# Sequence transform with the tables stationary, so that z comes by token at once

## The chip, the cores and the metric

The kernel runs on one core of one Trainium2 chip. The metric is device time in microseconds (us) of one execution, taken as the median of repeated runs. The core has five engines with queues of their own: TensorE (PE in the profile, its weight loads PEld), VectorE (DVE), ScalarE (ACT), GpSimd (POOL) and SyncE (SP), which here issues DMAs. ACT issues a few DMAs too. SBUF is the working memory of 128 partitions; PSUM, in eight banks, is what TensorE writes to.

## The reference, cut to what matters

```python
def _attn_ref(x):                       # x: 8 x 3072 x 256
    X = np.fft.fft(x, axis=1)           # sequence transform
    X = np.fft.fft(X, axis=2)
    return X.real

def _moe_ref(x, w_in, w_out):           # w_in 256 x 2048, w_out 2048 x 256
    h = x @ w_in
    return (h - np.tanh(h)) @ w_out

def _moe2_ref(x, phi, w1, w2):          # phi 256 x 32, 8 experts of 4 slots
    logits = x @ phi
    d = softmax(logits over tokens)
    slot_input = d.T @ x
    ...                                 # small expert MLPs on 32 slots
    c = softmax(logits over slots)
    return c @ slot_out

reference(x, ...) = _moe2_ref(_moe_ref(_attn_ref(x).reshape(8 * 3072, 256), ...), ...)
```

The second transform (over 256 columns) and the residual form of the middle stage are folded into weights before the main loop, so that the loop needs `z`, the sequence transform of `x`, and applies the wide weights to `z`.

## The kernel before, in words

**Stages.** A head (to about 100 us) loads and folds the weights. The main loop goes over 8 batches of 12 tiles of 128 tokens. A tail from about 1275 us runs the experts and writes the output from saved logits.

**The sequence transform** has two steps. `dft24(b)` adds and subtracts the 24 slices of a batch in the buffer `xb` (operations "P" at L337 on POOL, "A" at L341 on ACT). Since x is real, a slice can hold both sides of the transform: the columns 0 to 128 of a slice hold cosine sums, the columns 129 to 255 sine sums, and column 128 belongs to the cosine side. Then `z_dft(i)` multiplies two slices `U` and `V` with the tables `C` and `Sn` of one tile (L421 to L424) on TensorE.

**One tile before.** `z_dft` has the slices stationary and streams the tables, so its PSUM bank `zps` holds z with columns on partitions (two halves of 128 columns, by 128 tokens). Its halves are columns 0 to 127 and 128 to 255, while the cosine side ends with column 128: so `trade` in `dft24` exchanges column 128 of `U` and `V` by three small ACT copies over `tC` (or `tD`), 15 of them a batch. From `zps`, `z_high` (L451, ACT) makes a rounded float32r copy and `z_low` (L455, DVE) the rest; both lie in the tile `zh`. `z_copy` (L441, ACT) copies `zps` to `z32`, `z_turn` (L460) transposes it on TensorE to `tps`, and `z_turned` (L464, ACT) copies that to `zts`, z by token.

**Four groups of a tile.** A tile has four groups g of 512 wide columns. `wide(g, 0)` and `wide(g, 1)` (L472) are three matmuls each, into `pp` and `qq`, with `zh` stationary. `evac` (L486, DVE) makes `pb` from `pp` and the column `zts[:, 129]`; `plus` (L491, DVE) makes the first half of `h` from `pb` and `qq`, `minus` (L494, POOL) the second from `pb` and the first. `act_h` (L499) is the tanh, back to PSUM, `act_t` (L507) its scaled float16 copy in the ring `tr`, `low_t` (L511, DVE) the float16 rest. Then `turn_t` (L515) issues one DMA transpose of 512 KB on SP's queue, `tt<-tr`, and `logits(g)` (L566, for a tile's first group L559 and L560 ahead of it, with `zh`) uses `tt` as stationary. For a pair of tiles softmax steps follow (L597 to L678), and `slots(i)` (L674, `ta<-tr,dh`) for a tile.

**Rings.** `zh` has 2 buffers, `zts` 5, `tt` 4, `pb` 3, `h` 2; `pp` and `qq` may hold 3 banks each of 7 that all share.

**Order.** Nothing is scheduled at run time: a planner (`Flow`) sets each engine's order when the program is built. Each operation has a due time (the offsets `SCHED` in units of groups, `4 * i + SCHED[...]` for a tile) and costs by engine; the planner takes, within a window of 40 operations, what can begin first. The loads of the next batch's `x` (8 a batch, issued by ACT at L307) are due every `XSTEP` groups. Each engine then runs its instructions strictly in that order.

Of the kernel before, what the change touches and what calls it, by code (L numbers as in the profile page):

```python
# [9 lines left out]
F32 = mybir.dt.float32  # L10
# [37 lines left out]
SCHED = {
    "soft_t": 13.585, "logits": 6.021, "slots": 16.891, "soft_d": 14.305, "z_slots": 16.295, "z_turn": -2.11,
    "wide0": -0.087, "wide1": 0.708, "z_dft": -5.872, "ls_sum": 13.142, "soft_m": 13.838, "soft_h": 15.611,  # L50
    "soft_l": 16.611, "z_acc": 20.073, "evac": 2.52, "z_high": -4.001, "z_low": -3.917, "z_copy": -3.035,
    "z_turned": 2.466, "low_t0": 5.48, "low_t1": 5.512, "plus": 2.954, "minus": 4.457, "soft_e": 13.941,
    "ls_keep": 13.542, "act_h0": 4.372, "act_h1": 5.168, "act_t0": 5.041, "act_t1": 5.277, "acc_add": 21.793,
    "soft_x": 13.523,
# [16 lines left out]
ZT = 5  # L71
# [164 lines left out]
def fft_mlp_softmoe_kernel(ctx: ExitStack, tc: tile.TileContext, x, w_in, w_out, phi, w1, w2, cq, fd, cm, ct, out):  # L236
# [33 lines left out]
    z3p = sbp("z3p", 1)  # L270
# [51 lines left out]
    tC = tmp.tile([128, 3, 4], F32, name="tC")  # L322
    tD = tmp.tile([128, 2], F32, name="tD")

    def dft24(b):
# [34 lines left out]
        c128 = slice(128, 129)  # L360

        def trade(sets, u, v, m):
            ns_, kk = sets.stop - sets.start, [("c", u)]
            ua, va = (lambda w=w: x4()[:, sets, w:w + m, c128] for w in (u, v))
            ta = lambda: tC[:, 0:ns_, 4 - u:4 - u + m, None]
            ku, kv = ([("x", b % 2, 8 * q + w + e) for q in range(sets.start, sets.stop) for e in range(m)] for w in (u, v))
            A(0, (kk, ta), (ku, ua), 1.0)
            A(0, (ku, ua), (kv, va), 1.0)
            A(0, (kv, va), (kk, ta), 1.0)

            vs = lambda: x4()[:, sets, v:v + m, 129:256]
            A(0.5 * ns_ * m, (kv, vs), (kv, vs), -1.0)

        for r in range(3):
            q = 8 * r
            t = tA if r % 2 == 0 else tB
            P(4, T(t, 0, 4), X(q, 4), X(q + 4, 4), add)
            P(4, X(q + 4, 4), X(q, 4), X(q + 4, 4), sub)
            P(2, X(q + 2, 2), T(t, 0, 2), T(t, 2, 2), sub)
            P(2, T(t, 0, 2), T(t, 0, 2), T(t, 2, 2), add)  # L380
            P(1, T(t, 2), X(q + 5), X(q + 7), sub)
            P(1, T(t, 3), X(q + 5), X(q + 7), add)
            A(2, T(t, 2, 2), T(t, 2, 2), float(np.sqrt(0.5)))
            P(1, X(q), T(t, 0), T(t, 1), add)
            P(1, X(q + 1), T(t, 0), T(t, 1), sub)
            P(2, X(q + 5, 2, 2), X(q + 4, 2, 2), T(t, 2, 2), add)
            P(2, X(q + 4, 2, 2), X(q + 4, 2, 2), T(t, 2, 2), sub)
            if r == 0:
                trade(slice(0, 1), 4, 6, 2)
                trade(slice(0, 1), 2, 3, 1)  # L390
                dft24.first = len(ops)
        for r, h, n, t in ((4, 6, 2, tA), (2, 3, 1, tB)):
# [21 lines left out]
    def z_dft(i):  # L414
# [38 lines left out]
    def z_low(i):  # L453
        z = zs[i]
        nv.tensor_tensor(out=z[2], in0=zpp[i], in1=z[1].bitcast(F32), op=ALU.subtract)  # L455

    def z_turn(i):
        tps = zpp[i] = halves(bank(f"zq{i}", "tps", 256))
        for k in range(2):
            nt.transpose(tps[:, k, :], zs[i][0][:, k, :], eye)  # L460
# [559 lines left out]
    hf.add({"A": 0.36}, lambda _: z_high(0), ["z0"], ["z2"])  # L1020
    hf.add({"V": 0.39}, lambda _: z_low(0), ["z0", "z2"], [("zh", 0)])
    hf.add({"A": 0.5}, lambda _: z_copy(0), ["z0", ("zh", 0), "clear"], ["z1"], free="B:zp0 B:sp0")
    hf.add({"T": 0.2}, lambda _: z_turn(0), ["z1"], ["z3"], take="B:zq0")
    hf.add({"A": 0.3}, lambda _: z_turned(0), ["z3"], [("zt", 0)], free="B:zq0")
# [190 lines left out]
    per_tile(z_high, {"A": 0.27}, lambda i: ([("zp", i)], [("zi", i)], "", ""))
    per_tile(z_low, {"V": 0.34}, lambda i: ([("zp", i), ("zi", i)], [("zh", i)], "", ""))
    per_tile(z_copy, {"A": 0.27}, lambda i: ([("zp", i), ("zh", i)], [("z", i)] + ["spec"] * (i % NQ == 0), "z32", f"z B:zp{i}" + f" B:sp{i}" * (i % NQ == 0)))
    per_tile(z_turn, {"T": 0.22}, lambda i: ([("z", i)], [("zq", i)], f"+B B:zq{i}", "z32"))
    per_tile(z_turned, {"A": 0.27}, lambda i: ([("zq", i), ("zh", i)], [("zt", i)], "zt", f"B:zq{i}"))
# [7 lines left out]
    stage(minus, n4, 1, {"G": 1.24}, lambda g: ([("pb", g), ("h", g, 0)], [("h", g, 1)], "", "pb"))  # L1227
# [15 lines left out]
    for g in sorted({*range(n4)} - {*by_pe}):  # L1243
        put(g + 0.001, {"D": 2.58}, lambda e, g=g: turn_t(g), [("t1", g, 0), ("t1", g, 1)], [("tt", g)], "tt", "", 2.4, "low_t1")
# [118 lines left out]
    fl = Flow({"B": 7, "w": WB, "v": WB, "z": 1, "a": 1, "z32": 1, "zh": 2, "zt": ZT, "pb": PB, "h": HB, "t": TB, "tt": 4, "L": 1, "dT": 1,  # L1363
# [322 lines left out]
```

## Time and profile before

| | us |
|---|---|
| median of 3 runs | 1377.36 |
| lowest and highest of them | 1374.88, 1383.24 |
| the profiled execution, first to last instruction (its span) | 1375.7 |
| PE, DVE, ACT, POOL busy in it | 1288.9, 1242.7, 1130.1, 1134.0 |

The page gives the profiled execution's span; no time around it is listed, and it lies 1.7 us under the median of the runs. A wait in the profile is the idle time of an engine ahead of one of its instructions, put down to what ended last. Matmuls overlap, so the duration of one is longer than what it takes from the next: the cost on the path is read from the starts.

### The profile page before, as it was taken

What the parts mean: (1) busy time and instruction counts of PE and PEld (TensorE: products, weight loads), DVE (VectorE), ACT (ScalarE), POOL (GpSimd) and SP (SyncE); (2) the same over time, 40 slices, a digit from 0 to 9 for tenths busy, and PEclk for the clock granted to TensorE, in tenths of its full rate; (3) what the DMA queues carried; (4) which work ended last, traced back from release to release, by engine and by line L of the source; (5) the groups of instructions that cost most, each with busy time, mean ns of one, the idle gap of its engine ahead of it and who ended that gap; (6) DMA issues with size and microseconds to landing.
All of it is one profiled execution on the core that took longest, in us unless ns stands there. A gap on an engine that the chain in (4) does not pass through costs nothing.

```text
span 1375.7 us, 37397 instructions
## 1 busy us (share of the span) xinstructions
PE 1288.9 (94%) x14155; PEld 939.9 (68%) x14155; DVE 1242.7 (90%) x2248; ACT 1130.1 (82%) x2520; POOL 1134.0 (82%) x869
## 2 busy tenths in 40 slices
PE   4888999999999899999999999999999999999895
PEld 3666676776777676777777767776777776667484
DVE  7789898999999898999999999999999999889394
ACT  3448887989999787998899889888899898787494
POOL 5956899999999898999999999999999994333352
PEclk9999999999999999999999999999999999999998
DMA  8349999999999999999999999999999999999989
GB/s 275 123 155 186 185 195 214 191 204 198 220 190 200 182 186 197 189 213 190 224 191 192 199 212 196 206 188 217 183 197 203 200 206 212 199 188 263 339 346 387
DMA packets 848483, 290.23 MB, mean 211 GB/s; under 512 B 793264, under 2 KB 837168, under 8 KB 847408
## 3 DMA queue, kind: packets, MB, share of 16 engines
q1 hardware_dynamic: 822192, 265.82, 102.1%
q10 hardware_dynamic: 26112, 22.03, 5.7%
q8 instruction: 111, 1.82, 0.5%
q14 instruction: 68, 0.56, 0.1%
HBM read 58.15 MB, written 30.67 MB: 65 GB/s over the span
## 4 chain that ended last, share of the span: by engine, by line
PE 69%; DMA 21%; DVE 4%; ACT 2%; issue 1%; POOL 1%; SPq 0%; DVEq 0%; ACTq 0%; POOLq 0%
DMA tt<-tr 20%; PE qq L472 16%; PE pp L472 15%; PE L L566 10%; PE ta L674 8%; PE tps L1594 3%; PE tps L460 1%; PE hps L911 1%; PE zlp L658 1%; PE zps L421 1%; PE zps L422 1%; PE zps L423 1%; PE zps L424 1%; PE hps L880 1%; PE L L559 1%
## 5 line engine op out<-in xcount | busy, mean ns | idle before, releaser
L494 POOL TENSOR_TENSOR h<-pb,h 128x512 f32<-128x512 f32 x384 | 495.6, 1296 | 130.4 <-DVE h L491 121.5
L499 ACT ACTIVATE th<-h 128x512 f32<-128x512 f32 x768 | 457.2, 611 | 78.5 <-DVE h L491 36.0
L511 DVE SCALAR_TENSOR_TENSOR tr<-th,tr 128x512 f16<-128x512 f32 x768 | 515.1, 682 | 3.8 <-ACT tr L507 2.8
L507 ACT ACTIVATE tr<-th 128x512 f16<-128x512 f32 x768 | 443.9, 603 | 7.4 <-DVE lsw L578 1.2
L472 PE MATMUL qq<-Wh,zh 128*128 128x512 f32 x768 | 337.5, 439 | 0.7 <-DVE tr L511 0.3
L472 PE MATMUL pp<-Wh,zh 128*128 128x512 f32 x768 | 324.1, 422 | 0.9 <-ACT tr L872 0.4
L486 DVE SCALAR_TENSOR_TENSOR pb<-W,zts,pp 128x512 f32<-128x512 f32 x384 | 283.8, 739 | 13.4 <-PE pp L472 6.3
L491 DVE SCALAR_TENSOR_TENSOR h<-pb,qq 128x512 f32<-128x512 f32 x384 | 260.8, 679 | 27.0 <-PE qq L472 16.6
L566 PEld LDWEIGHTS <-tt 128*128 128x128 f16 x6144 | 195.8, 96 | 105.8 <-DMA tt<-tr 55.3
L566 PE MATMUL L<-WPn,tt 128*128 128x64 f16 (+1 forms) x6144 | 231.0, 185 | 39.0 <-DMA tt<-tr 38.4
L472 PEld LDWEIGHTS pp<-Wh,zh 128*128 128x128 f32 x768 | 145.3, 189 | 69.5 <-issue 14.4
L472 PEld LDWEIGHTS qq<-Wh,zh 128*128 128x128 f32 x768 | 146.1, 190 | 28.9 <-issue 5.3
L472 PE MATMUL pp<-Wl,zh 128*128 128x512 f32 x384 | 152.6, 397 | 0.0
L472 PE MATMUL qq<-Wl,zh 128*128 128x512 f32 x384 | 152.3, 397 | 0.0
L674 PE MATMUL ta<-tr,dh 128*32 128x512 f16 x2304 | 143.0, 383 | 0.0
L337 POOL TENSOR_TENSOR xb<-xb 128x508 f32<-128x508 f32 (+3 forms) x98 | 137.7, 1409 | 5.4 <-DVE xb L337 5.0
L337 POOL TENSOR_TENSOR tA<-xb 128x1024 f32<-128x1024 f32 (+2 forms) x68 | 104.7, 1548 | 17.2 <-DMA xb<-in_x 15.0
L674 PEld LDWEIGHTS <-dh 128*32 128x32 f16 x2304 | 53.2, 96 | 75.6 <-issue 33.9
L337 POOL TENSOR_TENSOR xb<-tA 128x508 f32<-128x508 f32 (+2 forms) x77 | 82.1, 1073 | 0.2
L472 PEld LDWEIGHTS pp<-Wl,zh 128*128 128x128 f32 x384 | 73.4, 191 | 7.9
L337 POOL TENSOR_TENSOR tB<-xb 128x1024 f32<-128x1024 f32 (+1 forms) x45 | 71.8, 1602 | 8.3 <-DVE tB L337 7.6
L337 POOL TENSOR_TENSOR xb<-xb,tA 128x512 f32<-128x512 f32 (+1 forms) x46 | 77.2, 1678 | 0.2
(267 smaller groups left out, 1919.6 us busy)
## 6 DMA issues: line engine op xcount, KB each, us to landing
xb<-in_x ACTq DMA_DIRECT2D x24, 512.0 KB, 6.4
tr<-in_moe_w SPq DMA_DIRECT2D x16, 512.0 KB, 8.9
xb<-in_moe_w SPq DMA_DIRECT2D x12, 512.0 KB, 4.6
tt<-tr SPq DMA_TRANSPOSE x380, 5.6
raw<-in_moe_w_in SPq DMA_DIRECT2D x8, 512.0 KB, 6.1
raw<-in_moe_w_out SPq DMA_DIRECT2D x8, 512.0 KB, 4.2
xb<-in_x SPq DMA_DIRECT2D x8, 512.0 KB, 8.2
out<-tr SPq DMA_DIRECT2D x4, 1024.0 KB, 10.4
```

The costliest lines, as they stand in the source:

```text
L337: fn = lambda e: e.tensor_tensor(out=out[1](), in0=a[1](), in1=c[1](), op=op)
L421: nt.matmul(zps[:, 0, :], xb[:, U, 0:128], C, start=True, stop=False)
L472: nt.matmul(o, z, v, start=n == 0, stop=n == 2)
L486: nv.scalar_tensor_tensor(out=pb, in0=W128[:, c, :], scalar=zs[i][3][:, 129:130], in1=pqs.pop((g, 0)), op0=ALU.mult, op1=ALU.add)
L491: nv.scalar_tensor_tensor(out=hs[g][:, 0, :], in0=pbs[g], scalar=0.5, in1=pqs.pop((g, 1)), op0=ALU.mult, op1=ALU.add)
L494: ng.tensor_tensor(out=hs[g][:, 1, :], in0=pbs.pop(g), in1=hs[g][:, 0, :], op=ALU.subtract)
L499: ns.activation(out=o, in_=hs[g][:, k, :], func=AF.Tanh)
L507: ns.activation(out=place_t(g)[:, 0, k], in_=ths[g, k], func=AF.Copy, scale=T14)
L511: nv.scalar_tensor_tensor(out=t[:, 1, k], in0=ths.pop((g, k)), scalar=T14, in1=t[:, 0, k], op0=ALU.mult, op1=ALU.subtract)
L566: nt.matmul(L[:, pm].rearrange("p b s -> p (b s)")[:, 0:n], tt[:, hl, pm, f, :], WPn[:, 4 * c + f].rearrange("p b s -> p (b s)")[:, 0:n], ...
L674: nt.matmul(tas[p][32 * c:32 * c + 32, :], dhl[p][:, dl, 2 * k + pm, :], ts[c][:, tl, pm, :], start=(k == 0 and n == 0), stop=(i == tiles( ...
L1594: nt.matmul(o.rearrange("p r d -> p (r d)"), c[:, j, :], R[:, 3 * h + k:3 * h + k + 2, :].rearrange("p r d -> p (r d)"), start=(h == 0), s ...
```

## The change

`z_dft` now has the tables stationary and streams the slices, 129 columns for the cosine side and 127 for the sine side, so `zps` holds z by token. `z_copy` copies it to `zts` at once; `z_turn` transposes `zts` on TensorE, and `z_high` and `z_low` read the transposed bank. `z_turned` and the tile `z32` are gone, and so are the three copies of each `trade` (what is left, `turned`, is the change of sign that stood in it). A `zh` buffer is now taken at `z_turn` and no longer at `z_dft`; `zts` has 6 buffers. Planner costs of `z_turn`, `z_copy`, `minus` and the DMA transpose are higher, and all due times are new.

```diff
-XLEAD = 6.425
-XSTEP = 5.269
-XAT = -23.453
+XLEAD = 8.366
+XSTEP = 6.655
+XAT = -23.637
...
-    "wide0": -0.087, "wide1": 0.708, "z_dft": -5.872, "ls_sum": 13.142, "soft_m": 13.838, "soft_h": 15.611,
+    "wide0": -0.777, "wide1": -0.557, "z_dft": -7.091, "ls_sum": 12.873, "soft_m": 14.028, "soft_h": 16.03,
...
-ZT = 5
+ZT = 6
...
-        def trade(sets, u, v, m):
-            ns_, kk = sets.stop - sets.start, [("c", u)]
...
-            A(0, (kk, ta), (ku, ua), 1.0)
-            A(0, (ku, ua), (kv, va), 1.0)
-            A(0, (kv, va), (kk, ta), 1.0)
+        def turned(sets, v, m):
+            ns_ = sets.stop - sets.start
+            kv = [("x", b % 2, 8 * q + v + e) for q in range(sets.start, sets.stop) for e in range(m)]
             vs = lambda: x4()[:, sets, v:v + m, 129:256]
             A(0.5 * ns_ * m, (kv, vs), (kv, vs), -1.0)
...
-            nt.matmul(zps[:, 0, :], xb[:, U, 0:128], C, start=True, stop=False)
-            nt.matmul(zps[:, 0, :], xb[:, V, 0:128], Sn, start=False, stop=True)
-            nt.matmul(zps[:, 1, :], xb[:, U, 128:256], Sn, start=True, stop=False)
-            nt.matmul(zps[:, 1, :], xb[:, V, 128:256], C, start=False, stop=True)
+            nt.matmul(zps[:, 0:129], C, xb[:, U, 0:129], start=True, stop=False)
+            nt.matmul(zps[:, 0:129], Sn, xb[:, V, 0:129], start=False, stop=True)
+            nt.matmul(zps[:, 129:256], C, xb[:, V, 129:256], start=True, stop=False)
+            nt.matmul(zps[:, 129:256], Sn, xb[:, U, 129:256], start=False, stop=True)
...
-        zs[i][0] = z3p.tile([128, 2, 128], F32, tag="z32", name="z32")
-        ns.copy(out=zs[i][0], in_=zpp.pop(i))
+        zs[i] = [None, None, None, zts[:, i % ZT, :]]
+        ns.copy(out=zs[i][3][:, 1:257], in_=zpp.pop(i))
...
+            nt.transpose(tps[:, k, :], zs[i][3][:, 1 + 128 * k:129 + 128 * k], eye)
...
-    def z_turned(i):
-        zs[i][3] = zts[:, i % ZT, :]
-        ns.copy(out=zs[i][3][:, 1:257], in_=zpp.pop(i).rearrange("p a b -> p (a b)"))
...
-    stage(minus, n4, 1, {"G": 1.24}, lambda g: ([("pb", g), ("h", g, 0)], [("h", g, 1)], "", "pb"))
+    stage(minus, n4, 1, {"G": 1.29}, lambda g: ([("pb", g), ("h", g, 0)], [("h", g, 1)], "", "pb"))
...
-        put(g + 0.001, {"D": 2.58}, lambda e, g=g: turn_t(g), [("t1", g, 0), ("t1", g, 1)], [("tt", g)], "tt", "", 2.4, "low_t1")
+        put(g + 0.001, {"D": 2.72}, lambda e, g=g: turn_t(g), [("t1", g, 0), ("t1", g, 1)], [("tt", g)], "tt", "", 2.4, "low_t1")
```

**The order of the instructions, place 1.** On TensorE in the middle of the main loop, where the logits of a tile begin: the tile whose `zh` stands at L559 (L536 in the changed kernel) is one tile behind that of the wide matmuls. Before:

```order
L472 MATMUL qq_9095<-Wh_84,zh_8929 128x512
L472 MATMUL qq_9095<-Wl_85,zh_8929 128x512
L472 MATMUL qq_9095<-Wh_84,zh_8929 128x512
L472 MATMUL pp_9104<-Wh_84,zh_8929 128x512
L472 MATMUL pp_9104<-Wl_85,zh_8929 128x512
L472 MATMUL pp_9104<-Wh_84,zh_8929 128x512
L559 MATMUL L_8869<-Al_115,zh_8715 128x128
L560 MATMUL L_8869<-Al_115,zh_8715 128x2x32
```

The same place now:

```order
L449 MATMUL pp_9851<-Wh_84,zh_9681 128x512
L449 MATMUL pp_9851<-Wl_85,zh_9681 128x512
L449 MATMUL pp_9851<-Wh_84,zh_9681 128x512
L449 MATMUL qq_9859<-Wh_84,zh_9681 128x512
L449 MATMUL qq_9859<-Wl_85,zh_9681 128x512
L449 MATMUL qq_9859<-Wh_84,zh_9681 128x512
L536 MATMUL L_9631<-Al_112,zh_9478 128x128
L537 MATMUL L_9631<-Al_112,zh_9478 128x2x32
```

In both, the `pp` is that of the third group of its tile. Before, the `qq` ahead of it is that of the second group; now `pp` and `qq` of one group stand together, and the logits follow the `qq` of the third group.

**Place 2.** On ACT in the middle of the main loop, the copies of one tile between tanh (`th<-h`) and its float16 copy (`tr<-th`). Before:

```order
L499 ACTIVATE th<-h 128x512
L451 CAST zh<-zps 128x256
L507 ACTIVATE tr<-th 128x512
L499 ACTIVATE th<-h 128x512
L441 COPY z_9198<-zps 128x256
L507 ACTIVATE tr<-th 128x512
L499 ACTIVATE th<-h 128x512
L464 COPY zts<-tps 128x256
L507 ACTIVATE tr<-th 128x512
L499 ACTIVATE th<-h 128x512
L341 ACTIVATE xb_76<-tC 128x2
L507 ACTIVATE tr<-th 128x512
```

Now, at another tile (`zts<-zps` is the copy of a later tile than `zh<-tps`; the DMA is a load of the next batch's x):

```order
L422 COPY zts<-zps 128x256
L484 ACTIVATE tr<-th 128x512
L476 ACTIVATE th<-h 128x512 x2
L306 DMA xb_76<-in_x 128x2x256
L484 ACTIVATE tr<-th 128x512
L437 CAST zh<-tps 128x256
```

Two copies a tile are left of three, and the small copies over `tC` are gone; `zts` is written more than a tile ahead of its use.

**Place 3.** On TensorE in the changed kernel, between the transposes of a tile (`tps<-cms,zts`) and its first wide matmuls (`zh_9915`), a stretch with the slots of an earlier tile in it:

```order
L449 MATMUL pp_9896<-Wh_84,zh_9681 128x512
L431 MATMUL tps_9905<-cms_109,zts_105 128x128 x2
L449 MATMUL qq_9911<-Wh_84,zh_9681 128x512
...
L543 LDWEIGHTS tt_9819
...
L651 LDWEIGHTS dh_9730
...
L449 MATMUL pp_9973<-Wh_84,zh_9915 128x512
```

Before, this was the distance from a tile's `zps` to its first wide matmuls:

```order
L424 MATMUL zps_9149<-cqs_113,xb1_76 128x128
L472 MATMUL pp_9159<-Wh_84,zh_8929 128x512
...
L566 LDWEIGHTS tt_9031
...
L472 MATMUL qq_9190<-Wh_84,zh_8929 128x512
...
L472 MATMUL pp_9200<-Wh_84,zh_9167 128x512
```

What stands between the bank that `zh` is made from and the first use of `zh` is one `qq`, one block of logits and one of slots now, and was a `pp`, a block of logits and a `qq`; on the other tile of each pair it is a `pp`, a `qq`, a block of logits and two small softmax matmuls now.

## Rows read from the trace of the kernel before

**Rows 1.** Page, chain that ended last, shares of the span by engine and line

```profile
PE 69%; DMA 21%; DVE 4%; ACT 2%; issue 1%; POOL 1%; SPq 0%; DVEq 0%; ACTq 0%; POOLq 0%
```

**Rows 2.** Busy time by stage: PE, PEld, DVE, ACT, POOL, clock, DMA share, GB/s

```profile
100.00:1130.00 1030.00, 994.13 (x11478) 730.89 (x11478) 970.45 (x1747) 909.50 (x2050) 976.59 (x747) 0.99 1.14 198
1130.00:1275.00 145.00, 139.26 (x1726) 99.00 (x1724) 130.00 (x241) 117.10 (x251) 54.30 (x43) 1.00 1.11 218
```

**Rows 3.** TensorE's instructions in order of time: start, duration, line

```profile
1040.75 1.48 PE L674 MATMUL ta<-tr,dh 128*32 128x512 f16 x24
1042.16 0.50 PE L472 MATMUL pp<-Wh,zh 128*128 128x512 f32 x1
...
1042.97 0.60 PE L566 MATMUL L<-WPn,tt 128*128 128x64 f16 x16
1043.41 0.48 PE L472 MATMUL qq<-Wh,zh 128*128 128x512 f32 x1
...
1044.20 0.40 PE L472 MATMUL pp<-Wh,zh 128*128 128x512 f32 x1
...
1044.90 0.22 PE L559 MATMUL L<-Al,zh 128*128 128x128 f32 x1
```

**Rows 4.** Waits of the whole span: total us, times, longest us

```profile
PEld L566 <- DMA tt<-tr: 55.3, 61, 4.1
...
PE L L566 <- DMA tt<-tr: 38.4, 37, 3.9
...
DVE pb L486 <- ACT zts L464: 5.3, 8, 2.0
```

**Rows 5.** Waits from 100 to 1130 us

```profile
POOL h L494 <- DVE h L491: 45.7, 42, 3.4
...
PE L L566 <- DMA tt<-tr: 33.2, 29, 3.9
```

**Rows 6.** The tile tt: issue times min/median/max ns, landing times

```profile
L515 SPq DMA_TRANSPOSE tt<-tr x379: 1316/2651/5997, 102.4 to 1255.1; - x190
...
DMA to landing us min/median/max: 4.2/5.6/10.1
```

**Rows 7.** The longest such wait: timeline of ACT's, SP's and TensorE's queues

```profile
459.84 0.44 ACTq L307 DMA_DIRECT2D xb<-in_x  x1
...
463.09 6.00 SPq L515 DMA_TRANSPOSE tt<-tr  x1
...
469.46 0.82 PE L566 MATMUL L<-WPn,tt 128*128 128x64 f16 x16 [3.89 <-DMA tt<-tr]
...
471.68 2.75 PE L674 MATMUL ta<-tr,dh 128*32 128x512 f16 x24
```

**Rows 8.** Busy time in the 20 us around it, columns as in rows 2

```profile
460.00:470.00 10.00, 6.11 (x73) 5.05 (x73) 7.73 (x13) 7.98 (x18) 9.63 (x8) 0.90 1.24 159
470.00:480.00 10.00, 10.00 (x99) 6.43 (x96) 5.95 (x12) 4.13 (x9) 5.50 (x4) 0.75 0.93 180
```

**Rows 9.** Groups by form: count, busy us, mean ns, idle before

```profile
L464 ACT COPY zts<-tps 128x256 f32<-128x256 f32 x96 | 37.1, 387 | 12.1 <-PE tps L460 11.8
```

**Rows 10.** L341: small ACT copies, count, min/median/max ns

```profile
L341 ACT ACTIVATE tC<-xb x32: 187/205/282, 66.1 to 1134.5; 128x2 f32<-128x2 f32 x16, 128x1 f32<-128x1 f32 x8, 128x4 f32<-128x4 f32 x8
```

**Rows 11.** From a tile's zps to its first wide matmul, timelines of three engines

```profile
1046.50 0.38 PE L421 MATMUL zps<-cqs,xb 128*128 128x128 f32 x2
...
1047.17 0.39 PE L424 MATMUL zps<-cqs,xb 128*128 128x128 f32 x2
1047.31 0.47 PE L472 MATMUL pp<-Wh,zh 128*128 128x512 f32 x1
...
1049.33 0.40 PE L472 MATMUL pp<-Wh,zh 128*128 128x512 f32 x1
...
1048.23 0.37 ACT L451 CAST zh<-zps 128x256 fp32r<-128x256 f32 x1
...
1048.72 0.41 DVE L455 TENSOR_TENSOR zh<-zps,zh 128x256 fp32r<-128x256 f32 x1
```

**Rows 12.** POOL's work in the loop, 300 to 1100 us

```profile
L494 POOL TENSOR_TENSOR h<-pb,h 128x512 f32<-128x512 f32 x265 | 341.5, 1294 | 30.4 <-DVE h L491 26.3 <-ACT z L441 1.6 <-ACT tr L507 0.9
```

More of the change, by code (lines that the diff above doesn't have):

```diff
@@ L38 @@
 NQ = 12
-DSTEPS = 32.998
-XLEAD = 6.425
-XSTEP = 5.269
-XAT = -23.453
+DSTEPS = 33.347
+XLEAD = 8.366
+XSTEP = 6.655
+XAT = -23.637
 XBUSY = 1.25
 XLAT = 5.0
-XFIRST = 24.735
+XFIRST = 26.264
 SCHED = {
-    "soft_t": 13.585, "logits": 6.021, "slots": 16.891, "soft_d": 14.305, "z_slots": 16.295, "z_turn": -2.11,
-    "wide0": -0.087, "wide1": 0.708, "z_dft": -5.872, "ls_sum": 13.142, "soft_m": 13.838, "soft_h": 15.611,
[L51 to L54, printed above, removed]
+    "soft_t": 13.884, "logits": 5.754, "slots": 16.828, "soft_d": 14.997, "z_slots": 16.764, "z_turn": -6.044,
+    "wide0": -0.777, "wide1": -0.557, "z_dft": -7.091, "ls_sum": 12.873, "soft_m": 14.028, "soft_h": 16.03,
+    "soft_l": 16.693, "z_acc": 20.81, "evac": 1.167, "z_high": -5.502, "z_low": -4.279, "z_copy": -6.26,
+    "low_t0": 4.839, "low_t1": 5.286, "plus": 3.095, "minus": 3.3, "soft_e": 14.131,
+    "ls_keep": 12.969, "act_h0": 3.982, "act_h1": 3.863, "act_t0": 4.399, "act_t1": 4.607, "acc_add": 23.511,
+    "soft_x": 13.019,
 }
@@ L445, in z_copy, with z_turn @@
             ns.copy(out=spec[0:1, 1, b:b + 1], in_=sps[0:1, 1:2])
+    def z_turn(i):
+        tps = zpp[i] = halves(bank(f"zq{i}", "tps", 256))
+        for k in range(2):
+            nt.transpose(tps[:, k, :], zs[i][3][:, 1 + 128 * k:129 + 128 * k], eye)
     def z_high(i):
@@ L454, in z_low @@
         z = zs[i]
[L455 to L460, printed above, removed]
-    def z_turned(i):
-        zs[i][3] = zts[:, i % ZT, :]
-        ns.copy(out=zs[i][3][:, 1:257], in_=zpp.pop(i).rearrange("p a b -> p (a b)"))
+        nv.tensor_tensor(out=z[2], in0=zpp.pop(i), in1=z[1].bitcast(F32), op=ALU.subtract)
     hs, tq, tts, pqs, pbs, ths = {}, {}, {}, {}, {}, {}
@@ L1019, in fft_mlp_softmoe_kernel @@
     hf.add({"T": 1.0}, lambda _: z_dft(0), ["cq"] + x_keys(0), ["z0"], take="B:zp0 B:sp0")
[L1020 to L1024, printed above, removed]
+    hf.add({"A": 0.5}, lambda _: z_copy(0), ["z0", "clear"], ["z1", ("zt", 0)], free="B:zp0 B:sp0")
+    hf.add({"T": 0.3}, lambda _: z_turn(0), ["z1", "cms"], ["z3"], take="B:zq0")
+    hf.add({"A": 0.36}, lambda _: z_high(0), ["z3"], ["z2"])
+    hf.add({"V": 0.39}, lambda _: z_low(0), ["z3", "z2"], [("zh", 0)], free="B:zq0")
     hf.run()
@@ L1211, in k_dft @@
         n = i % NQ
-        return [("cq", n)] + x_keys(i), [("zp", i)], f"+B zh z B:zp{i}" + f" B:sp{i}" * (n == 0), ""
+        return [("cq", n)] + x_keys(i), [("zp", i)], f"+B z B:zp{i}" + f" B:sp{i}" * (n == 0), ""
     per_tile(z_dft, {"T": 0.9}, k_dft)
[L1215 to L1219, printed above, removed]
+    per_tile(z_copy, {"A": 0.3}, lambda i: ([("zp", i)], [("zt", i)] + ["spec"] * (i % NQ == 0), "zt", f"z B:zp{i}" + f" B:sp{i}" * (i % NQ == 0)))
+    per_tile(z_turn, {"T": 0.3}, lambda i: ([("zt", i)], [("zq", i)], f"+B zh B:zq{i}", ""))
+    per_tile(z_high, {"A": 0.27}, lambda i: ([("zq", i)], [("zi", i)], "", ""))
+    per_tile(z_low, {"V": 0.34}, lambda i: ([("zq", i), ("zi", i)], [("zh", i)], "", f"B:zq{i}"))
     n4 = last + 1
```

34 lines of the change are left out of this document (9 added, 25 removed).

## The prediction

> **What bounds the kernel now.** I read the chain that ended last first: 69% of it is TensorE and 21% DMA, nearly all of that the transposes `tt<-tr`; ACT has 2% [rows 1]. So the first question is not what ACT saves but what TensorE waits for. The busy times by stage come next. From 100 to 1130 us TensorE is busy for 994 of 1030 us, POOL for 976.6 and ACT for 909.5; after 1130 us POOL has little left to do (54 of 145 us), because the last batch needs no transform after it [rows 2]. A busy TensorE says little by itself, so I read its instructions in order of time: an undisturbed stretch has no hole. A block of slots takes 1.41 us (1040.75 to 1042.16), `pp` 0.81 behind it, a block of logits 0.44, `qq` 0.79 and the `pp` behind it 0.70 [rows 3]. The chain of TensorE is therefore dense, and its holes are in the list of waits: the logits waited 37 times, 38.4 us in total, for a DMA transpose (61 times, 55.3 us, on the side of the weight loads, which includes times in which matmuls still ran) [rows 4]. 33.2 us of the 38.4 fall before 1130 us [rows 5]. POOL's own waits in that stretch are 45.7 us, for `plus` [rows 5]: it runs at 95% and idles when the wide matmuls come late.
>
> Why do transposes come late? SP needs 2.65 us (median) to issue one of the 379 and up to 6.0; a transpose lands after 5.6 us, up to 10.1 [rows 6]. The longest wait shows the pattern: ACT issues a load of x at 459.84, the next transpose occupies SP for 6.0 us from 463.09, and at 469.46 the logits have waited 3.89 us [rows 7]. There TensorE stood idle for 4 us; the granted clock then was 0.75 on average from 470 to 480 us [rows 8], a mixture of 2.4 and 1.2 GHz, and a block of slots took 2.75 us where it takes 1.48 by the same kind of row [rows 3, 7]. Over 100 to 1130 us the clock is 0.99 [rows 2], so some 10 us of full speed are lost that way, part of them while TensorE waits anyway.
>
> **The change, part by part.**
>
> *ACT.* Gone are 96 copies `z_turned` at 387 ns, 37.1 us [rows 9], and 15 small copies a batch, 120 in all, at the 205 ns that 32 of them show [rows 10]: 24.6 us. Together 61.7 of ACT's 1130 us. The `z_copy` that stays writes `zts` instead of `z32`, the same 128 by 256 elements. As ACT has 2% of the chain, nearly all of the 61.7 us lie beside other work. On the path is what waited for `zts`: `evac` 8 times, 5.3 us [rows 4]; with `zts` written more than a tile ahead this goes. I take 3 us, between 0 and 5.3.
>
> *TensorE's work.* Four table matmuls a tile with 129, 129, 127 and 127 streamed columns in place of four with 128, and two transposes as before: the same 512 columns. The stationary loads are four either way. The twelfth tile of a batch has four matmuls in place of six small ones. I set this at 0; the bounds are 0 and a gain of 2 us. An odd count of columns is not in the trace; the four table matmuls of 128 columns take 0.81 us (1046.50 to 1047.31) [rows 11], so 0.2 us for 128 columns, and one more or less is nothing.
>
> *Logits later.* This is the main term. Counted over both orders, the logits of a group stand behind the `pp` of the same later group as before, but now also behind its `qq`, so that between `qq` of a group and its logits there are one more `qq` and one more block of logits: 0.79 + 0.44 = 1.23 us [rows 3]. The other end moves too: on DVE `low_t`, which the transpose waits for, has on average 0.12 to 0.17 of a group more of `plus` and `evac` ahead of it. A group takes 3.0 us (265 of them in 800 us [rows 12]), so 0.4 us of the 1.2 are used up there. A transpose gets 0.8 us more to land. Taken from 37 waits of 1.04 us on average this would be 30 us if each lost the full 0.8 and 0 if DMA simply landed later by as much; many waits are shorter than 0.8, and one that is shortened lets the next start earlier. I take 23 us.
>
> *Loads of x.* They are spread over 6.7 groups each in place of 5.3; in ACT's order the last four of a batch now take about 12 groups and took 9. Since the longest wait stood behind such a load [rows 7], fewer of them should pile up: 4 us, between 0 and 10.
>
> *Clock.* If the longest waits lose 0.8 us and some vanish, part of the 10 us comes back: 3 us, between 0 and 8.
>
> *z's path.* `zh` is now made from the transposed bank, so the head's first tile needs `z_copy` and the transposes ahead of `z_high`: the copy at 0.39 us [rows 9], the transposes at half of four table matmuls, 0.4 us [rows 11], and two hops between engines, once: +1 us. In the loop the cover decides. Before, from the last table matmul (1047.17 plus 0.39) to the end of `z_low` (1048.72 plus 0.41) were 1.57 us, and the first wide matmul of that tile began 0.20 us later, at 1049.33 [rows 11]: tight already. In the new order there are between the transposes and that matmul, on one tile of a pair, `qq`, logits and slots (0.79 + 0.44 + 1.41 = 2.6 us), on the other `pp`, `qq`, logits and two small matmuls (at least 0.70 + 0.79 + 0.44 = 1.9 us); before it was 0.81 + 0.44 + 0.79 = 2.0 us here [rows 3]. About the same, so 0; what it costs if the cover is too thin is a rival below.
>
> *POOL.* Its work in the loop stays. In the head four short operations move to it from DVE, at some 1 us each: at most 4 us, hidden if POOL is not late there.
>
> *Sum.* On TensorE's side −23 − 4 − 3 − 3 + 1 = −32 us. Before 1130 us POOL puts a ceiling on it: its work fills 976.6 of 1030 us, so at most 53 us can go, and of these 45.7 are waits for `plus` [rows 2, 5]. Two engines at 95% do not idle at the same moments, and what one of them gains the other gives back in part. I take two thirds: −21 us. The profiled execution spans 1375.7 us, the median of the runs is 1.7 above; 1377.4 − 21 gives 1356 us.
>
> **The rivals.**
>
> *No change.* POOL is the real bound up to 1130 us, and TensorE's waits only move: what it no longer waits for at the logits it waits for at `pp` and `qq`, whose banks come free when POOL's half of `h` has gone through ACT. For it: POOL's 95%, and that its work is not touched [rows 2]. Against it: of its 53 idle us 45.7 are waits for something that TensorE feeds [rows 5]. What remains is the last stretch, with 5.2 us of logits waits (38.4 − 33.2), and `evac`: 1372 to 1379 us. The Trainium skill, "Perfetto Trace Analysis", section "Identifying the Most-Contended Engine", judges TensorE's headroom by the share of its weight loads and would optimize the busiest engine first; here weight loads fill 731 of 1030 us, 71%, which leaves POOL as that engine and this change without an object [rows 2]. By the starts in [rows 3] TensorE has no such headroom, so the trace agrees with the rule only in POOL's share.
>
> *More than forecast.* Every wait for a transpose goes, and most of the lost clock: 38.4 + 6 + 3 − 1 = 46 us, POOL's ceiling just met: 1331 us. Against it: waits of 3.9 us do not go with 0.8 us.
>
> *Slower.* The place is the first `pp` of a tile. ACT runs its queue in order, and `z_high` can stand behind a tanh and its copy. If ACT reaches `z_high` one instruction of 0.6 us late on the tile with 1.9 us of cover (1.57 us are needed), TensorE stalls 0.3 us; two late, 0.9 us. At 0.6 us on average on 48 tiles this is 29 us, and it delays everything behind it on TensorE, so that the gain on the logits is halved: 1377 + 29 − 11 = 1395 us. It decides if `z_low` ends more than 1.9 us behind the transposes. Against it: ACT has 62 us less to do.
>
> That the change does not do what it says is no rival: the orders show the copies gone and the logits moved.
>
> **How the numbers follow.** My forecast (1345 to 1363) has a chance of 0.53, more than forecast 0.1, no change 0.25, slower 0.12. The range reaches from 1333, near the case in which all waits go, to 1381, the end of no change with the spread of the runs; about 0.2 is left out, most of it above. One per cent, 14 us, is about what a measurement of this kernel can tell from no change. Faster by more: 0.63; within: 0.25; slower by more: 0.12.
>
> **What would show it.** In the changed profile ACT's busy time should be near 1070 us; the waits of the logits for `tt<-tr` well below 38.4 us, some 15, with POOL's wait for `plus` before 1130 us near 25; `evac` should not wait for `zts`. If the logits waits fall and the time stays, POOL or `pp` will show new waits and the first rival holds. If the first `pp` of a tile waits for DVE, the slower one does. If the logits wait as much as before, the transposes land later because they are issued later, and the step on the logits is wrong.

## The result, and the profile after

The changed kernel takes 1358.4 us (median of 4 runs, 1354.4 to 1362.0), the kernel before 1377.8 in the same comparison: ratio 0.9867, 95% interval 0.982 to 0.9915, so 18 us less (12 to 25). The profiled execution spans 1356.8 us. The forecast was 1356.

The page's chain that ended last, shares of the span by engine, changed kernel:

```profile
PE 54%; DMA 18%; DVE 11%; POOL 6%; ACT 5%; issue 4%; SPq 0%; ACTq 0%; DVEq 0%; POOLq 0%
```

TensorE's and the transposes' shares are smaller than in [rows 1], and DVE, POOL and ACT now have 22% of the chain. The busy times from 100 to 1130 us, columns as in [rows 2]:

```profile
100.00:1130.00 1030.00, 992.33 (x11658) 744.52 (x11659) 986.08 (x1781) 895.53 (x1896) 986.27 (x754) 0.99 1.15 201
```

More is done in the same 1030 us: TensorE executes 1.6% more instructions, in 1.8 us less busy time, and POOL 754 for 747. The stage is faster, but no engine has become free except ACT. The waits of the whole span:

```profile
POOL h L471 <- DVE h L468: 96.4, 62, 8.5
...
PEld L543 <- DMA tt<-tr: 51.0, 58, 2.5
...
PE L L543 <- DMA tt<-tr: 30.5, 33, 2.0
DVE pb L463 <- PE pp L449: 22.7, 33, 3.4
```

The logits (now L543) still wait 30.5 us for transposes; it was 38.4 [rows 4]. The longest wait is 2.0 us in place of 3.9. `evac` no longer waits for `zts`, but longer for `pp`: 22.7 us, where it was 6.3. From 100 to 1130 us, against [rows 5]:

```profile
PE L L543 <- DMA tt<-tr: 27.7, 31, 1.9
POOL h L471 <- DVE h L468: 27.3, 32, 4.2
```

POOL waits 27.3 us for `plus`, and waited 45.7. The tile `tt` (issue times, then landing, as in [rows 6]):

```profile
L543 PE MATMUL L<-WPn,tt x6144: 176/189/277, 110.7 to 1252.4; 128*128 128x64 f16 x100, 128*128 128x32 f16 x99
L492 SPq DMA_TRANSPOSE tt<-tr x379: 1315/2767/6244, 103.3 to 1236.0; - x190
...
DMA to landing us min/median/max: 4.3/5.4/10.0
```

The first of these rows also says when the first and the last logits started; I call that stretch the loop: 1141.7 us here. The same row of the kernel before:

```profile
L566 PE MATMUL L<-WPn,tt x6144: 177/189/277, 108.7 to 1270.6; 128*128 128x64 f16 x100, 128*128 128x32 f16 x99
```

That is 1161.9 us: the 20 us were gained in the loop. A transpose takes no less time to issue than before, and lands hardly sooner (5.4 us in the median, it was 5.6).

What became of TensorE's idle time can be read from its busy time in the loop (PE comes first, columns as in [rows 2]; the profile models the ends of matmuls). First before, then now:

```profile
108.70:1270.60 1161.90, 1121.00 (x13146) 821.60 (x13146) 1091.44 (x1970) 1018.07 (x2281) 1024.21 (x784) 0.99 1.14 200
```

```profile
110.70:1252.40 1141.70, 1099.33 (x13102) 821.17 (x13102) 1086.27 (x1971) 981.43 (x2076) 1025.07 (x785) 0.99 1.15 204
```

TensorE was idle for 40.9 us of the loop and is idle for 42.4 now. The logits wait 7.9 us less for transposes, and 9.4 us came back in many small waits elsewhere. All of the 20 us lie in TensorE's busy time, which fell by 21.7 us.

TensorE's work also changed. Groups of the wide matmuls, before and after (count, busy us, mean ns):

```profile
L472 PE MATMUL qq<-Wh,zh 128*128 128x512 f32 x768 | 337.5, 439 | 0.7 <-DVE tr L511 0.3 <-DVE pb L486 0.2
L472 PE MATMUL pp<-Wh,zh 128*128 128x512 f32 x768 | 324.1, 422 | 0.9 <-ACT tr L872 0.4 <-DVE tr L511 0.3
```

```profile
L449 PE MATMUL pp<-Wh,zh 128*128 128x512 f32 x768 | 336.6, 438 | 4.4 <-DVE pb L463 1.5 <-ACT tr L484 0.9 <-ACT tr L849 0.4
L449 PE MATMUL qq<-Wh,zh 128*128 128x512 f32 x768 | 313.7, 408 | 1.2 <-DVE tr L488 0.5 <-DVE zh L441 0.2
```

The same 1536 matmuls take 11 us less. TensorE's timeline in the changed kernel shows one reason:

```profile
1043.22 0.60 PE L543 MATMUL L<-WPn,tt 128*128 128x64 f16 x16
1043.67 0.47 PE L449 MATMUL pp<-Wh,zh 128*128 128x512 f32 x1
1043.99 0.39 PE L449 MATMUL pp<-Wl,zh 128*128 128x512 f32 x1
1044.21 0.39 PE L449 MATMUL pp<-Wh,zh 128*128 128x512 f32 x1
1044.44 0.40 PE L449 MATMUL qq<-Wh,zh 128*128 128x512 f32 x1
1044.68 0.39 PE L449 MATMUL qq<-Wl,zh 128*128 128x512 f32 x1
```

The first matmul of `pp`, behind a block of logits, takes 0.32 us to the next start; the first of `qq`, directly behind `pp`, takes 0.24. In the old order `pp`, logits, `qq`, slots stood in turn; in the new one `pp` and `qq` stand together and nearly all else in one gap. Counted in the loop of both traces, 561 wide blocks stood behind something that was no wide block, and 420 do now. A wide block ahead of slots, or of another block with 32 stationary columns, costs 0.09 us more too; there were 100 of these and are 45. The two counts at these prices make some 16 us (141 times 0.08, 55 times 0.09). That is an estimate; the rest of the 21.7 us is not accounted for one by one.

### The profile page after: what moved, and what is told of

The parts are those of the page before. It is cut to its first block, busy times and chain, and to the rows that moved or that the text cites. A ratio compares the mean times of both kernels' runs of the same rounds, so it can differ in the third digit from the quotient of the medians.

```text
span 1356.8 us, 36880 instructions
## 1 busy us (share of the span) xinstructions
PE 1270.2 (94%) x14123; PEld 942.5 (69%) x14123; DVE 1236.7 (91%) x2245; ACT 1092.0 (80%) x2303; POOL 1136.4 (84%) x873
## 4 chain that ended last, share of the span: by engine, by line
PE 54%; DMA 18%; DVE 11%; POOL 6%; ACT 5%; issue 4%; SPq 0%; ACTq 0%; DVEq 0%; POOLq 0%
DMA tt<-tr 17%; PE pp L449 12%; PE qq L449 10%; PE L L543 8%; PE ta L651 7%; DVE tr L488 3%; PE tps L1569 3%; POOL h L471 3%; DVE pb L463 3%; DVE h L468 2%; DMA xb<-in_x 2%; ACT th L476 2%; ACT tr L484 1%; PE zps L405 1%; PE hps L888 1%
## 5 line engine op out<-in xcount | busy, mean ns | idle before, releaser
L449 PE MATMUL pp<-Wh,zh 128*128 128x512 f32 x768 | 336.6, 438 | 4.4 <-DVE pb L463 1.5
L449 PE MATMUL qq<-Wh,zh 128*128 128x512 f32 x768 | 313.7, 408 | 1.2 <-DVE tr L488 0.5
L463 DVE SCALAR_TENSOR_TENSOR pb<-W,zts,pp 128x512 f32<-128x512 f32 x384 | 283.6, 739 | 24.2 <-PE pp L449 22.7
L543 PEld LDWEIGHTS <-tt 128*128 128x128 f16 x6144 | 191.7, 96 | 113.7 <-issue 62.0
L543 PE MATMUL L<-WPn,tt 128*128 128x64 f16 (+1 forms) x6144 | 230.3, 185 | 31.1 <-DMA tt<-tr 30.5
L449 PEld LDWEIGHTS qq<-Wh,zh 128*128 128x128 f32 x768 | 145.7, 190 | 38.4 <-DVE tr L488 4.2
L651 PEld LDWEIGHTS <-dh 128*32 128x32 f16 x2304 | 59.4, 97 | 51.8 <-issue 9.9
L449 PEld LDWEIGHTS qq<-Wl,zh 128*128 128x128 f32 x384 | 73.2, 191 | 12.7
L334 POOL TENSOR_TENSOR tB<-xb 128x256 f32<-128x256 f32 (+1 forms) x47 | 73.0, 1561 | 10.6 <-DVE tB L334 9.7
```

Source lines behind the costliest of these rows:

```text
L334: fn = lambda e: e.tensor_tensor(out=out[1](), in0=a[1](), in1=c[1](), op=op)
L449: nt.matmul(o, z, v, start=n == 0, stop=n == 2)
L463: nv.scalar_tensor_tensor(out=pb, in0=W128[:, c, :], scalar=zs[i][3][:, 129:130], in1=pqs.pop((g, 0)), op0=ALU.mult, op1=ALU.add)
L543: nt.matmul(L[:, pm].rearrange("p b s -> p (b s)")[:, 0:n], tt[:, hl, pm, f, :], WPn[:, 4 * c + f].rearrange("p b s -> p (b s)")[:, 0:n], ...
L651: nt.matmul(tas[p][32 * c:32 * c + 32, :], dhl[p][:, dl, 2 * k + pm, :], ts[c][:, tl, pm, :], start=(k == 0 and n == 0), stop=(i == tiles( ...
```

## The experiments

Three theories: (1) TensorE's shorter order; (2) fewer waits for transposes; (3) ACT's relief. All runs stand in this table; the ratio is to the kernel before, with its 95% interval; the waits are those of the logits for `tt<-tr` on TensorE in the whole span, the loop is the stretch above, and idle is what of the loop TensorE is not busy. These three are of the profiled execution, which lies up to 7 us off the median of its runs (furthest in e5, 7 us above).

| run | median us | ratio | waits us | loop us | idle us |
|---|---|---|---|---|---|
| before | 1377.8 | | 38.4 | 1161.9 | 40.9 |
| changed | 1358.4 | 0.9867 (0.982–0.9915) | 30.5 | 1141.7 | 42.4 |
| e1 | 1383.3 | 1.004 (1.0019–1.0061) | 33.6 | 1154.3 | 43.5 |
| e2 | 1430.2 | 1.0381 (1.035–1.0413) | 62.1 | 1195.7 | 74.0 |
| e3 | 1390.7 | 1.0112 (1.0074–1.0151) | 42.4 | 1158.2 | 45.2 |
| e4 | 1366.5 | 0.9918 (0.9891–0.9945) | 37.2 | 1147.9 | 47.4 |
| e5 | 1370.0 | 0.9965 (0.9942–0.9988) | 49.0 | 1161.6 | 55.2 |
| e6 | 1374.5 | 0.9989 (0.9963–1.0015) | 36.2 | 1159.3 | 38.9 |
| e7 | 1359.3 | 0.9889 (0.9858–0.992) | 25.7 | 1144.3 | 40.9 |
| e8 | 1342.1 | 0.9753 (0.9724–0.9781) | 12.5 | 1128.2 | 16.6 |
| e9 | 1335.9 | 0.9728 (0.9699–0.9758) | 7.9 | 1120.8 | 22.2 |
| e10 | 1375.7 | 1.0014 (0.9991–1.0037) | 37.0 | 1157.8 | 39.3 |
| e11 | 1394.9 | 1.0155 (1.0124–1.0186) | 49.0 | 1180.6 | 57.4 |
| e12 | 1356.3 | 0.987 (0.9842–0.9898) | 27.6 | 1132.0 | 38.4 |

**e1, new path of z with the old offsets.**

```diff
-XSTEP = 6.655
+XSTEP = 5.269
...
-"logits": 5.754, "slots": 16.828, "wide0": -0.777, "wide1": -0.557
+"logits": 6.021, "slots": 16.891, "wide0": -0.087, "wide1": 0.708
```

> The changed kernel (new path of z, no column 128 exchanged, ACT relieved of the 62 us) with the offsets of the kernel before for every step that is not one of z's, and its spacing of the loads of x. Theory 1, TensorE's own order: a wide block (pp or qq) that stands behind a block of short float16 matmuls costs 0.08 us more than one behind another wide block, and a wide block ahead of slots 0.09 us more; there were 561 entries into a wide block from something else and are 420 in the changed kernel, 497 here. Summed over the order with the start-to-start times of the two traces, TensorE's loop is 1004 us in the kernel before, 978 in the changed one, 989 here; so some 1367 us. Theory 2, waits for the transposes: logits stand behind pp again, so their waits should be near the 38.4 us of before and the time near 1366 us. Theory 3, ACT's relief and the new path of z: these stay, so 1358 us.

The time is 5 us above that of before, against all three. But the new order has a hole behind the loop; waits of the whole span:

```profile
PE tps L1534 <- DVE cs L1527: 16.0, 1, 16.0
```

That wait stands in the tail, where neither kernel has more than 1.4 us of it: one edit of offsets moves the planner's order everywhere. The loop itself ended 13 us earlier (last logits at 1257.6) and took 7.6 us less. So the new path of z without the new offsets has some of the gain; the total says nothing of it.

**e2, old path of z with the new offsets.**

```diff
-"logits": 6.021, "wide0": -0.087, "wide1": 0.708, "z_dft": -5.872, "z_high": -4.001
+"logits": 5.754, "wide0": -0.777, "wide1": -0.557, "z_dft": -7.272, "z_high": -5.401
```

> The kernel before (three ACT copies a tile, column 128 exchanged) with the offsets of the changed kernel for every step that is not one of z's, and its spacing of the loads of x; z's own steps are 1.4 groups earlier so that they are done in time. Theory 1, TensorE's own order: 409 entries into a wide block, TensorE's loop 980 us by the same sum, so some 1360 us although ACT still has its 62 us. Theory 2, waits for the transposes: logits stand behind qq as in the changed kernel, waits near 30 us, 1360 us to 1370. Theory 3, ACT's relief: none here, so 1378 us.

3.8% slower: the loop took 34 us more although only 409 wide blocks stand behind something that is no wide block. TensorE's idle time rose by 33 us, 24 of them the logits' waits, now 62.1 us; its busy time in the loop, 1121.7 us, did not fall, at a granted clock of 0.98 in place of 0.99. The tail has the hole too (13.5 us). `z`'s offsets are my own here, so this does not show what a fit could reach on the old path; it shows that few such entries alone do not make the kernel fast.

**e3, before with the slots moved.**

```diff
-"slots": 16.891, "z_slots": 16.295, "z_turn": -2.11, "z_dft": -5.872
+"slots": 17.03, "z_slots": 17.02, "z_turn": -1.98, "z_dft": -5.97
```

> The kernel before with only four offsets changed, none of them the logits' or a wide block's: slots 16.891 to 17.03, z_slots 16.295 to 17.02, z_turn -2.11 to -1.98, z_dft -5.872 to -5.97, so that TensorE has slots and z's pieces in the gap in which the logits are, and not between qq and pp. Theory 1, TensorE's own order: 497 entries into a wide block in place of 561, TensorE's loop 989 us in place of 1004, so 1365 to 1370 us. Theory 2, waits for the transposes: logits stand where they stood, 38 us of waits, 1378 us. Theory 3, ACT's relief: none, 1378 us.

Again a hole of 16.0 us in the tail. The loop took 3.7 us less, and I had expected 15 from the order: TensorE's busy time in it fell by 8.0 us, to 1113.1, and its idle time rose by 4.3, nearly all of it waits of the logits (4.0).

**e4, the changed kernel with earlier logits.**

```diff
-"logits": 5.754
+"logits": 5.33
```

> The changed kernel with the logits' offset 5.33 in place of 5.754: they stand behind pp in most groups, and a transpose has some 0.4 of a group, 1.2 us, less to land. Theory 1, TensorE's own order: there are more entries into a wide block (495 for 420), but fewer other switches, and the sum over the order is the same 977 us; so 1358 us, within 5. Theory 2, waits for the transposes: the logits' waits come back to 40 us or more, 1370 to 1380 us. Theory 3, ACT's relief: unchanged, 1358 us.

No hole here. 1366.5 us: between the theories. From the end of `low_t` to the start of its logits the median is 9.05 us here, 9.08 before and 9.86 in the changed kernel, so a transpose has as long to land as before. The waits are 37.2 us, nearly those of before, while TensorE's busy time stays that of the changed kernel (1100.5 us for 1099.3). So by the ratios some 11 of the 18 us stay without the later logits, and some 7 go with them. The intervals of e4 and of the changed kernel overlap, so the 7 us are a size, not a proof; the loop, 6 us longer in the profile, agrees.

In e5 to e9 and e12 every instruction keeps its place: work is taken away or doubled where it stands, and the planner changes nothing.

**e5, before with less work for TensorE.**

```diff
-        passes(o, zh[:, n, :], zl[:, n, :], (Wh[:, n, fs], Wl[:, n, fs]))
+        passes(o, zh[:, n, :], zl[:, n, :], (Wh[:, n, fs], Wl[:, n, fs]), 2 if n and g % 3 == 1 else 3)
```

> The kernel before, every instruction in its order, with the third of the three passes left out of qq in every third group (128 passes of 768; their output lacks z's low half there). TensorE has 128 times 0.23 us, 29 us, less to do, about as much as the changed kernel's order saves it by the sum over the orders (28 us); ACT, POOL and the places of the logits are untouched. Theory 1, TensorE's own work is what the change saved: 1350 to 1360 us, as the changed kernel. Theory 2, the change saved waits for transposes: shorter groups leave a transpose less time to land, so part of the 29 us turns into waits of the logits, which rise from 38 us to 45 or more, and the time is 1365 to 1378 us. Theory 3, ACT's relief: nothing changes at ACT, 1377 us.

Of 29 us of work 5 us (2 to 8) are seen, and in the profiled execution, one of the slowest of e5, the loop is as long as before: TensorE's busy time fell by 14.6 us and its idle time rose by 14.3. The waits of the logits for transposes, whole span of e5:

```profile
PEld L566 <- DMA tt<-tr: 69.4, 68, 5.1
...
PE L L566 <- DMA tt<-tr: 49.0, 43, 4.9
```

38.4 became 49.0 us: TensorE arrives sooner and waits longer. So less work for TensorE, with nothing else changed, gives little in the kernel before, and TensorE by itself was not its bound. It does not show what the order gave in the change, where `z`'s path and the offsets changed with it: in e4, with waits like those of before, most of the order's gain stayed.

**e6, before with less work for ACT.**

```diff
+        c = slice(0, 256) if i < 2 * ZT else slice(128, 136)
-        ns.copy(out=zs[i][3][:, 1:257], in_=zpp.pop(i).rearrange("p a b -> p (a b)"))
+        ns.copy(out=zs[i][3][:, 1:257][:, c], in_=zpp.pop(i).rearrange("p a b -> p (a b)")[:, c])
...
-            A(0, (kk, ta), (ku, ua), 1.0)
+            A(0, (kk, ta), (ku, ua), 1.0, b == 0)
```

> The kernel before, every other instruction in its order, with ACT relieved by hand: from the eleventh tile on z_turned copies 8 of its 256 columns (0.2 us in place of 0.39), and the 105 small copies that exchange column 128 are left out after the first batch; the spectrum is wrong there. ACT has some 35 to 40 us less to do, 60% of what the change takes from it. Theory 3, ACT's relief: 60% of the change's 19 us, 1365 us or less. Theories 1 and 2: TensorE's order and the logits' places are those of before, so 1377 us, within 4.

**e7, the changed kernel with more work for ACT.**

```diff
-        ns.copy(out=zs[i][3][:, 1:257], in_=zpp.pop(i))
+        for k in range(2 if i else 1):
+            ns.copy(out=zs[i][3][:, 1:257], in_=zpp[i])
+        zpp.pop(i)
```

> The changed kernel, every other instruction in its order, with each copy of zts made twice (95 copies of 0.38 us, 36 us more work on ACT, as much as z_turned took). Theory 3, ACT's relief: most of the gain goes, 1370 us or more. Theories 1 and 2: ACT's copies lie beside other work, 1358 to 1361 us.

Ratios 0.9989 and 0.9889: taking 22 us of busy time from ACT (1108.4 us of 1130.1) gains nothing that can be measured, giving back 29 us (1121.3 for 1092.0) loses nothing. I had expected 35 to 40 and 36, from the durations of the copies; durations on ACT overlap, so its busy time moved by less. Theory 3, as far as it is ACT's time, falls.

**e8 and e9, both kernels without loads of x.**

```diff
-            load = lambda e, b=b, a=a, c=c, m=m: load_x(b, a, c, m)
+            load = lambda e, b=b, a=a, c=c, m=m: load_x(b, a, c, m) if b < 2 else None
```

> The kernel before, every other instruction in its order, without the loads of x for batches 2 to 7 (24 DMAs left out; these batches transform what stands in the buffer). Theory 2, waits for transposes, most of them behind loads of x: the logits' waits fall from 38 us to 15 or 20, the slow clock behind the longest goes, and the time falls by as much or more than the change gave, to 1350 or 1358 us. Theory 1, TensorE's own order: what the waits cost is mostly given back elsewhere, as in the changed kernel, where they fell by 8 us and other waits rose by more; 1368 to 1375 us. Theory 3: 1377 us.

> The changed kernel, every other instruction in its order, without the 48 loads of x for batches 2 to 7 (these batches transform what stands in the buffer). The same edit took 34 us from the kernel before, to 1342 us. Theory 2, the change saved waits for transposes, most of which loads make late: where no load comes in between, the two kernels should be about equally fast, 1335 to 1345 us. Theory 1, the shorter order on TensorE: its gain does not hang on the loads, so 1358 less 34, 1320 to 1328 us.

(48 DMAs are left out in e8 as well; 24 is the count of the largest ones.) The kernel before gains 34 us by ratio, the changed one 19. Without loads the two are 3 us apart by ratio (6 by the medians) and were 18. The intervals of e8 and e9 overlap. It is tempting to read from this that most of what the change gave hangs on the loads of x. The busy times from 300 to 1100 us do not allow it (columns as in [rows 2]); before, changed, e8, e9:

```profile
300.00:1100.00 800.00, 776.19 (x9042) 569.30 (x9041) 756.39 (x1362) 707.94 (x1597) 768.73 (x586) 0.99 1.15 199
300.00:1100.00 800.00, 776.22 (x9224) 582.15 (x9222) 769.55 (x1394) 699.02 (x1484) 780.90 (x598) 1.00 1.16 203
300.00:1100.00 800.00, 794.94 (x9346) 583.45 (x9343) 778.75 (x1408) 731.78 (x1658) 791.42 (x610) 1.00 1.11 187
300.00:1100.00 800.00, 789.52 (x9370) 589.86 (x9370) 779.75 (x1416) 709.59 (x1506) 791.80 (x612) 1.00 1.12 188
```

POOL, the fifth engine of a row, is busy for 791 and 792 of 800 us in e8 and e9, that is 99% (TensorE is at 99% too). Both kernels have come to the end of POOL's idle time, so a shorter order on TensorE has hardly anything left to give there: in the loop TensorE's busy time is still 13 us less in e9 than in e8 (1098.6 for 1111.6), and its idle time 5.6 us more. So e8 and e9 show what the loads cost, 34 and 19 us, and not how the 18 us divide. The transposes that start between 300 and 1100 us, with their issue times; first e8, then e9:

```profile
L515 SPq DMA_TRANSPOSE tt<-tr x273: 1316/2348/5432, 299.1 to 1096.5; - x137
```

```profile
L492 SPq DMA_TRANSPOSE tt<-tr x276: 1316/2384/4909, 296.5 to 1098.8; - x138
```

The same stretch of before and of the changed kernel:

```profile
L515 SPq DMA_TRANSPOSE tt<-tr x266: 1327/2649/5997, 298.3 to 1098.8; - x133
```

```profile
L492 SPq DMA_TRANSPOSE tt<-tr x271: 1316/2702/6244, 300.0 to 1096.8; - x136
```

With loads a median issue is 0.3 us longer. The mean issue over groups 12 to 359, with the 0.1 us that SP leaves between two, against the time of a group: 2.88 of 3.03 us before (95%), 2.91 of 2.98 now (98%), 2.63 of 2.94 in e8 (89%), 2.67 of 2.92 in e9 (91%).

**e10, before with the new spacing of loads.**

```diff
-XSTEP = 5.269
+XSTEP = 6.655
```

(and the four numbers beside it)

> The kernel before with the changed kernel's five numbers for the loads of x and the transform behind them (XSTEP 6.655 for 5.269, XLEAD, XAT, XFIRST, DSTEPS), and nothing else. Logits stand where they stood; TensorE's order is nearly that of before (546 entries into a wide block for 561, 1002 us for 1004). If the spread of the loads is what the change gained by: 1358 to 1365 us. My prediction gave it 4 us: 1373. Theory 1: 1376 us. If the place of the logits decides: 1372 to 1377 us.

No difference. On the old path of z the spacing by itself gains nothing.

**e11, before with the logits later.**

```diff
-"logits": 6.021, "ls_sum": 13.142, "slots": 16.891
+"logits": 6.871, "ls_sum": 13.992, "slots": 17.741
```

> The kernel before with the offsets of the logits and of every step behind them (softmax, slots, sums) 0.85 of a group higher, 2.5 us, so that a transpose has that much more to land; the loads, the wide blocks and z's steps keep their offsets. TensorE's order gets shorter too (461 entries into a wide block, 994 us for 1004). Theory 2, waits for transposes: the logits' waits fall from 38 us below 15, and the time by as much, to 1350 or 1360 us. Theory 1, TensorE's order alone: 10 us less of its own work, of which a quarter counted where the logits kept their place: 1370 to 1375 us.

1.6% slower; the logits' waits rose to 49.0 us, against theory 2 as I put it. Another wait grew with them, against 5.3 us in [rows 4]:

```profile
DVE pb L479 <- ACT zts L457: 18.8, 18, 5.4
```

In the old path `zts` is made last, shortly ahead of `evac`, and what stands in front of `z_turn` on TensorE delays it. Later logits do not help there. That the late `zts` is why the logits wait more is only argued.

**e12, loads by row.**

```diff
+    def next_x(n):
+        for u in late_x[:n]:
+            load_x(*u)
+        del late_x[:n]
...
         ns.activation(out=place_t(g)[:, 0, k], in_=ths[g, k], func=AF.Copy, scale=T14)
+        next_x(k)
...
-            load = lambda e, b=b, a=a, c=c, m=m: load_x(b, a, c, m)
+            load = lambda e, b=b, a=a, c=c, m=m: load_x(b, a, c, m) if b < 2 else late_x.extend((b, a, c + k, 1) for k in range(m))
```

> The changed kernel, every other instruction in its order, with each load of x for batches 2 to 7 cut into its rows of 128 KB (one to four), and one row issued behind the second float16 copy of each group, so that a load of 512 KB takes four groups, 12 us, and not one piece. The same bytes are moved. If a load costs by its bytes alone: 1358 us, or a little more for ACT's 96 further issues. If it costs because it makes one transpose 3 us late, more than the logits' place leaves, while 0.7 us at each of four transposes is covered: 1340 to 1350 us, with the logits' waits below 20 us.

1356.3 us, not to be told from the changed kernel (0.987 and 0.9867). A median issue is 2.9 us (2.77), the longest landing 8.7 (10.0): the delay is spread, not removed. The loads seem to cost by their bytes; pieces of another size than these two were not tried.

## Why the prediction was right, and where its sum was not

The time was right by 2 us, and that was luck: the largest term was three times too large, and the part that by e4 gave most had been put at 0. I forecast that TensorE would wait less. Its idle time in the loop did not fall (40.9 and 42.4 us); its busy time did, by 21.7 us.

*Logits later (−23 us): the mechanism held, the size did not.* I forecast 0.8 us more for a transpose. From the end of `low_t` to the start of its logits the median went from 9.08 to 9.86 us, 0.78 more (groups 12 to 359). But landing came 0.72 later too (7.45 to 8.17 us behind `low_t`), because transposes now stand in line on SP: it starts one 2.61 us behind `low_t` in the median, and 1.60 before. So the waits fell by 7.9 us, not by 23, and by e4 the later logits are worth some 7. I treated the landing time as given, while it moved with the queue.

*TensorE's work (0, at most a gain of 2): wrong, and by e4 the larger part of the gain.* I counted streamed columns and not neighbours. [Rows 3] had the price: `qq` behind logits took 0.79 us, `pp` behind `qq` 0.70, and I used both numbers without asking how many blocks would change sides. TensorE's busy time fell by 21.7 us in the loop, of which the counted neighbours explain some 16, and by e4 some 11 of the 18 us remain when the logits are put back. By itself such work is worth less: in e5 about a sixth of its size.

*POOL's ceiling: it stands, but a second one was missed.* POOL's wait for `plus` came out as forecast (27.3, forecast 25), and e8 and e9 run into the ceiling itself: with the queue relieved the loop got 34 and 21 us shorter, until POOL was busy for 99% of the time from 300 to 1100 us. What I did not see is the queue of transposes: SP issued during 95% of a group's time before and 98% now. In the changed kernel both are nearly full, POOL for 780.9 of 800 us, which is 98% too. Which of them held the gain at 20 us stays open. The Trainium skill, "Perfetto Trace Analysis", section "What 'DMA-bound' means", names as one of its kinds an issuing engine whose track is solid with DMA work; SP's 98% is that kind. The Trainium skill's rule on the most-contended engine (same page, section "Identifying the Most-Contended Engine"), which I weighed under "no change", points to POOL, and the same trace has POOL as full.

*Loads of x (−4): 0 by their spacing (e10).* Their cost was far larger than I thought, 34 us in the kernel before (e8), but neither spacing nor smaller pieces take it away.

*Clock (−3) and `evac` (−3).* The clock from 100 to 1130 us is 0.99 as before. `evac`'s wait for `zts` went, and its wait for `pp` grew by 16.4 us to 22.7; e6 and e7 show that ACT's copies as such weigh nothing that can be measured, so that ACT's time lies beside other work was right. Its busy time fell by 38 us, not 62: the 62 were summed from durations, and these overlap on ACT (the 120 small copies last 25 us and add 8 to its busy time).

*Rivals.* "Slower" did not come: `pb` waits for `pp`, but the weight loads of `pp` waited for `z_low` 3 times, 1.4 us in total. "No change" fell by the interval, but its mechanism was half right: what TensorE no longer waits for at the logits it waits for elsewhere, so that its idle time is the same.

What is left open is the exact division of the 18 us. By e4 some 11 go to TensorE's order together with the new path of `z`, and some 7 to the later logits, without which the waits come back; the intervals leave room on both sides. Whether the order alone would give the 11 on the old path is not shown: e2 and e3 tried it by offsets, and neither got faster.

## What to carry to other kernels

A wait for a DMA need not be shortened by the time that its consumer is moved back when the queue that issues it is nearly full, as here: compare the issue time of all its DMAs with the time of a round first. Compare idle and busy time of the engine that you mean to relieve before you put a gain down to its waits. When two variants come out alike after a limit is lifted, look whether both have met the next limit. Count in a new order which blocks change their neighbour on TensorE, and price that by start-to-start times. When offsets of a planner are tried one at a time, look at the tail as well: three of six such edits here paid 14 to 16 us in a place that had nothing to do with the question.

## What the runs showed of the hardware

A wide float32 block of three matmuls directly behind another one takes 0.08 us less than behind a block of float16 logits (start to start 0.24 and 0.32 us for its first matmul). Loads of 18.9 MB on ACT's queue lengthened the issue of SP's transposes by 0.3 us in the median over the whole loop, and did so as much in pieces of 128 KB (e12: 2.9 us) as in pieces of up to 512 KB.
